# Attention and a dense block on one core: q and k stacked on 128 partitions, loaded by two queues and transposed in one step

## The chip, the cores and the metric

The kernel runs on one core of one Trainium2 chip. The metric is the device time of the kernel in microseconds (us). An engine is named here as the profile names it: PE (TensorE, the matrix engine), ACT (ScalarE), DVE (VectorE), POOL (GpSimd) and SP (SyncE, which in this kernel only issues DMAs). PSUM is the memory that PE writes to, in banks of 2 KB per partition; SBUF holds everything else on the core.

## What is computed

There are 8 batches of 8 heads with 576 tokens of 64 values. For each head, two attentions are added: one over tokens averaged in groups of four, whose result is repeated four times, and one over a band of plus and minus three tokens. The result, 4608 tokens of 512 values, goes through a dense block.

```python
q_d = q.reshape(B, H, Sd, factor, D).mean(axis=3)      # factor 4; k_d and v_d likewise
out_up = np.repeat(sm_attn(q_d, k_d, v_d), factor, axis=2)
mask = np.abs(pos[:, None] - pos[None, :]) < factor
scores = np.where(mask, scale * np.matmul(q, k.transpose(0, 1, 3, 2)), -1000000000.0)
out_local = np.matmul(softmax(scores), v)
x = (out_up + out_local).transpose(0, 2, 1, 3).reshape(B * S, H * D)
h = x @ w_in                                           # 512 -> 2048
out = (h - np.tanh(h)) @ w_out                         # 2048 -> 512
```

(`softmax` stands for the four lines of the reference that subtract the maximum, take the exponential and divide by the sum.)

## The kernel before

**The work.** Two heads make a pair, and there are 32 pairs, four to a batch. The function `attention` (line 373 on) writes down the steps of one pair. q and k of both heads are loaded as 32-bit values by `load_qk` (L286): each of 96 partitions holds six neighbouring tokens of both heads, so each row in memory is 1536 bytes; q and k lie beside each other in one tile `qkn` of four buffers. Two casts (L387) turn them to bf16 in `qr` (two buffers), one for q and one for k; each is 96 partitions by 768 elements. For each of q and k, six transposes on PE (L399) bring 96 x 128 to 128 x 96: q into the first PSUM bank of `ps_ts`, k into the second. After each, a copy on ACT (L405) of 128 x 576 puts the tokens in order into `qk`, with head 0 on partitions 0 to 63 and head 1 on 64 to 127.

From there on nothing is touched by the change: q and k are pooled in two additions (L416, L421), the scores of the first four query blocks (L434) go into the same `ps_ts`, ACT takes the exponential (L457) and DVE masks it (L460); then the scores of the last block and the pooled ones (L434, L449), two exponentials (L466, L469), a mask (L472), the product with v (L483, L489) into `ps_ox`, the division (L498, L500), seven transposes back (L510 to L514), and an addition (L519) into `xT`, the dense block's input. v is loaded by `load_v` (L305 to L311), cast (L346) and pooled on PE for two pairs at a time (L360, L362, copied by L367).

**The dense block.** Blocks of 512 tokens: 16 times four matmuls into one of four banks (L539), tanh on ACT (L547), a subtraction on DVE (L550), then 64 matmuls with w_out (L566) and a store (L577, L580). A block can begin when its batches' pairs are in `xT`. The weights are loaded as 32-bit values into tiles that are still unused (L323 to L332) and cast (L339).

**What sets the order.** `Program` is a planner in Python. Every step is put down with its engine, a cost in ns, what it reads and writes, and a priority; `order` plays the engines against each other and gives one order for each engine, which is then emitted as it is. Every engine works through its list in that order. Some steps (`choice`) name several engines, and the one that is free first in the plan gets them: the casts of q and k do (`REORDER`), with DVE for q and POOL for k after the first four pairs. DMAs are planned as one server with a cost for each kind (`T_QK`, `T_V`, `T_W`). Loads have a high priority: a load of q and k is issued as soon as the casts of four pairs before have freed the buffer, and all loads stand in one chain on SP, in the order in which they were put down. Dense work has the lowest priority on PE and fills what attention leaves. Before the first dense matmul, `filler` puts matmuls on a zero tile (L710) into planned gaps of PE.

The first four pairs use two sets of PSUM banks (`ps_ts`, `ps_ox` and `ps_ts1`, `ps_ox1`) in turn; after them, the second set is given to the dense block and all pairs share the first. In `ps_ts` the order is then: scores and exponential of pair p, transposes and copies of pair p+1, last scores of pair p.

Of the kernel before, what the change touches and what calls it, by code (L numbers as in the profile page):

```python
# [8 lines left out]
FP32 = mybir.dt.float32  # L9
# [141 lines left out]
def kernel(  # L151
# [17 lines left out]
    SCALE = 1.0 / float(D) ** 0.5  # L169
    A6 = 6  # L170
    G6 = S // A6
    QW = 120
# [10 lines left out]
    def fixed(name, shape, dt, n=None, pool=const):  # L183
        if n is None:
            return pool.tile(shape, dt, name=name, tag=name)
        return [pool.tile(shape, dt, name=f"{name}{i}", tag=f"{name}{i}")
                for i in range(n)]

    NQKN, NVST, NVW = 4, 6, 3
    ident = fixed("ident", [128, 128], BF16)  # L190
# [6 lines left out]
    w_out_sb = fixed("w_out_sb", [128, N_FF, Dm], BF16)  # L197
    qkn = fixed("qkn", [G6, 2, 2, A6 * D], FP32, NQKN)
    vst = fixed("vst", [128, 2, NT, 64], FP32, NVST)
    vw = fixed("vw", [128, 4, NT, 65], BF16, NVW)  # L200
    vd = fixed("vd", [128, 2, 4, 65], BF16, NVW)
    qr = fixed("qr", [G6, 2, A6, 128], BF16, 2)
    qk = fixed("qk", [128, 1192], BF16, 2)
# [72 lines left out]

    def load(ns, fn, keys, cost, pri):
        op("SP", ns, fn, writes=list(keys) + ["queue", ("q", keys[0])], pri=pri)
        op("DMA", cost, None, reads=[("q", keys[0])], writes=keys, pri=pri)

    def load_qk(p):

        b, h0, s = p // NP, 2 * (p % NP), p % NQKN
        for i, src in enumerate((q, k)):
            def issue(i=i, src=src):
                nc.sync.dma_start(  # L286
                    out=qkn[s][:, i], in_=src[b, h0:h0 + 2].rearrange(
                        "h (g a) d -> g h (a d)", a=A6))
            load(500, issue, [("qkn", s, i)], T_QK, -30)

    def load_v(p):

        b, j, s = p // NP, p % NP, p % NVST
        t = vst[s]
        for i in range(2):
            h = 2 * j + i
            base = v[b, h]

            def win(tok, n, nt, base=base):
                return bass.AP(tensor=base.tensor, offset=base.offset + tok * D,  # L300
                               ap=[[D, n], [QW * D, nt], [1, D]])

            def issue(h=h, i=i, win=win):
                if b == 0 and h == 0:
                    nc.sync.dma_start(out=t[4:128, i, 0, :], in_=v[b, h, 0:124, :])  # L305
                    nc.sync.dma_start(out=t[:, i, 1:5, :], in_=win(QW - 4, 128, 4))
                elif b == B - 1 and h == H - 1:
                    nc.sync.dma_start(out=t[0:100, i, 4, :], in_=v[b, h, 476:576, :])
                    nc.sync.dma_start(out=t[:, i, 0:4, :], in_=win(-4, 128, 4))
                else:  # L310
                    nc.sync.dma_start(out=t[:, i], in_=win(-4, 128, 5))  # L311
            if (b, h) in ((0, 0), (B - 1, H - 1)):
                def clear(h=h, i=i):
                    part = t[0:32, i, 0, :] if h == 0 else t[96:128, i, 4, :]
                    V.memset(part, 0.0)
                op("DVE", 100, clear, writes=[("vst", s, i)], pri=-99)
            load(1000, issue, [("vst", s, i)], T_V, -30)

# [54 lines left out]
    def attention(p):  # L373
# [5 lines left out]
        pri = 10 * p  # L379
        cold = 1.5 if p < NP else 1.0  # L380


        yield
        for i in range(2):
            dst = qr[s][:, i].rearrange("p a (h d) -> p h a d", d=D)
            srt = qkn[sn][:, i].rearrange("p h (a d) -> p h a d", d=D)
            P.choice([(eng, ns, lambda dst=dst, srt=srt, fn=fn: fn(out=dst, in_=srt))  # L387
                      for eng, ns, fn in REORDER[p >= NEARLY][i]],
                     reads=[("qkn", sn, i)], writes=[("qr", s, i)], pri=pri - 12)


        full = bass.AP(tensor=qk[s].tensor, offset=qk[s].offset,
                       ap=[qk[s].ap[0], [KOFF, 2], [1, 576]])
        for i in range(2):
            b16 = ps[:, i].bitcast(BF16)[:, 0:S]

            def tr(i=i, b16=b16):
                for a in range(A6):
                    T.transpose(b16[:, G6 * a:G6 * a + G6], qr[s][:, i, a, :],  # L399
                                ident[0:G6, 0:G6])  # L400
            if i == 0:
                P.fresh.add(len(P.ops))
            op("PE", 260 * cold, tr, reads=[("qr", s, i), "ident"],
               writes=[(t, i) for t in ts], pri=pri)
            op("ACT", 540, lambda i=i, b16=b16: A.copy(  # L405
                out=full[:, i].rearrange("p (g a) -> p g a", a=A6),
                in_=b16.rearrange("p (a g) -> p g a", a=A6)),
               reads=[(t, i) for t in ts], writes=[("qk", s, i)], pri=pri)
        ts = [(t, i) for t in ts for i in range(2)]
# [20 lines left out]

        def score(t, hh, c):
            rows = slice(64 * hh, 64 * hh + 64)
# [4 lines left out]
        def s1():  # L437
            for t in range(4):
                for hh in range(2):
                    score(t, hh, 512 * hh + QW * t)  # L440

        def s2():
            for hh in range(2):
                score(4, hh, 512 * hh)
            for i in range(2):
                for hh in range(2):
                    rows = slice(64 * hh, 64 * hh + 64)
                    c = 512 * hh + 96 + G * i
                    T.matmul(sc[:, c:c + G], qkd[s][rows, 1, 16 * i:16 * i + 128],  # L449
                             qkd[s][rows, 0, :], start=True, stop=True)  # L450
        qks = [("qk", s, i) for i in range(2)]
        yield
        op("PE", 420 * cold, s1, reads=qks, writes=ts, pri=pri)
        e1 = E[s][:, 0:960].rearrange("p (h c) -> p h c", h=2)
# [9 lines left out]
        yield  # L464
        op("PE", 380 * cold, s2, reads=qks + [("qkd", s)], writes=ts, pri=pri)
        op("ACT", 240, lambda: A.activation(  # L466
            out=e2v, in_=ps[:, :, 0:96], func=AF.Exp, scale=SCALE),
           reads=ts, writes=[("E", s, 1)], pri=pri)
        op("ACT", 560, lambda: A.activation(  # L469
            out=e3, in_=ps[:, :, 96:384], func=AF.Exp, scale=SCALE / 16.0),  # L470
           reads=ts, writes=[("E", s, 2)], pri=pri)
        op("DVE", 220, lambda: V.tensor_tensor(  # L472
# [3 lines left out]

        def outs():
# [25 lines left out]


        px = [po[:, i].bitcast(BF16) for i in range(2)]

# [76 lines left out]
    def dense(kb):  # L585
# [13 lines left out]
        for i in range(16):  # L599
            if kb < NBLK:  # L600
# [5 lines left out]
    ORDER = "p0p1p2p3"  # L606
    T_QK, T_V, T_W, W_PRI, NEARLY = 1150, 900, 2850, -3, NP
    CAST = [("POOL", 700, GP.tensor_copy), ("ACT", 520, A.copy)]
    CAST_V = [[("POOL", 720, GP.tensor_copy), ("ACT", 640, A.copy)],
              [("POOL", 720, GP.tensor_copy)]]  # L610
    any3 = [("DVE", 600, V.tensor_copy), ("ACT", 740, A.copy),
            ("POOL", 860, GP.tensor_copy)]
    REORDER = [[any3, any3], [any3[0:1], any3[2:3]]]
    ADDERS = [[("DVE", 700, 420, V), ("POOL", 1150, 750, GP)],
# [43 lines left out]

    def load_next():

# [3 lines left out]
        if queue:  # L664
            queue.pop(0)
        if nl[0] < NPAIR:
            load_qk(nl[0])
# [14 lines left out]
    for p in range(NPAIR):  # L682
# [10 lines left out]
        if p + 2 < NP:  # L693
            next(work[p + 2])
        load_next()
        if p % NP == NP - 1:
# [45 lines left out]
```

The softmax here doesn't subtract the row's maximum and nothing guards it: scores larger than these inputs give would overflow.

## Time and profile before

| what | value |
|---|---|
| two runs | 370.07 and 371.64 us, median 370.86 us |
| profiled execution: span from its first to its last instruction | 365.3 us (of its time only the span is recorded; the median of the runs is 5.6 us longer) |
| granted PE clock, mean | 0.995 |
| busy: PE, DVE, ACT, POOL | 348.1, 221.2, 222.2, 120.7 us |
| DMA: read from HBM, written | 37.74 MB, 9.44 MB |
| transposes of q and k (L399) | 360 of 96x96 into `ps_ts`, 24 into `ps_ts1` |
| copies of q and k (L405), 128x576 | 64, 640 ns in the median |
| casts of q and k (L387), 96x768 | DVE 541 to 1522 ns, POOL 818 to 2251 ns |
| first dense matmul | 31.72 us |
| last q, k and v load lands | about 180 us |

In lines of the profile, the number after an engine's name is the line of the kernel; `out<-in` are tiles, x is a count, and the bracket at the end gives the idle time of the engine ahead of it and what ended it. SPq stands for SP's instruction queue, which only issues DMAs: the time of such a line is that of the issue and not of the transfer. PEld is PE's loading of the stationary operand. Times are from the span's start.

### The profile page before, as it was taken

The numbers are of one execution on the slowest core, as the hardware profiler recorded it, in microseconds if no ns is written. First come the engines' busy times: TensorE is split into PE (matmuls) and PEld (weight loads), VectorE is DVE, ScalarE is ACT, GpSimd is POOL, SyncE is SP. The second block draws the span as 40 slices with busy tenths as digits, with TensorE's granted clock in tenths as the row PEclk, the third lists the DMA queues.
The fourth block names the chain that finished last, engine by engine and source line by source line (L and its number), as shares of the span: only waits on it lengthen the run. The fifth ranks groups of instructions, "written<-read, shape, count | busy, mean of one in ns | idle before, by whom it ended". The sixth has DMA issues, their size and how long they took to land.

```text
span 365.3 us, 7446 instructions
## 1 busy us (share of the span) xinstructions
PE 348.1 (95%) x2908; PEld 181.3 (50%) x2908; DVE 221.2 (61%) x362; ACT 222.2 (61%) x406; POOL 120.7 (33%) x156
## 2 busy tenths in 40 slices
PE   7777999999999999999999999999999999999995
PEld 3454455556555555555555555444444444444442
DVE  5786775688989988779777667434334334334300
ACT  3686986679787877777877774434434434434321
POOL 6744666674656564555635220000000000000000
PEclk9899999999999999999999999999999999999999
DMA  8999999999999986576400000010010011011012
GB/s 202 235 390 286 257 258 259 212 264 227 240 207 234 206 182 183 148 190 148 126 31 2 30 31 31 29 57 31 29 57 31 29 52 37 29 42 46 29 62 82
DMA packets 64816, 47.65 MB, mean 130 GB/s; under 512 B 43790, under 2 KB 56078, under 8 KB 64782
## 3 DMA queue, kind: packets, MB, share of 16 engines
q1 hardware_dynamic: 64782, 47.19, 54.1%
q8 instruction: 22, 0.36, 0.5%
q14 instruction: 12, 0.10, 0.1%
HBM read 37.74 MB, written 9.44 MB: 129 GB/s over the span
## 4 chain that ended last, share of the span: by engine, by line
PE 81%; DVE 6%; ACT 5%; DMA 3%; POOL 2%; issue 2%; SPq 0%; ACTq 0%; DVEq 0%; POOLq 0%
PE ps_hy_527 L566 9%; PE ps_hy_528 L566 9%; PE ps_hy_525 L539 8%; PE ps_hy_525 L566 8%; PE ps_hy_526 L539 8%; PE ps_hy_528 L539 7%; PE ps_hy_527 L539 7%; PE ps_hy_526 L566 7%; PE ps_ts L399 4%; PE ps_ts L434 3%; PE ps_ox L360 3%; DMA qkn_75<-in_k_dram 2%; ACT qk_91 L405 2%; PE ps_ox L483 2%; PE ps_ox L514 2%
## 5 line engine op out<-in xcount | busy, mean ns | idle before, releaser
L539 PEld LDWEIGHTS <-w_in_sb 128*128 128x128 bf16 x576 | 52.5, 98 | 59.6 <-issue 1.3
L566 PEld LDWEIGHTS <-gT_103 128*128 128x128 bf16 x320 | 28.9, 97 | 30.7
L566 PEld LDWEIGHTS <-gT_104 128*128 128x128 bf16 x256 | 23.5, 98 | 25.8
L405 ACT COPY qk_90<-ps_ts 128x576 bf16<-128x576 bf16 x32 | 19.5, 644 | 6.7 <-PE ps_ts L399 6.6
L416 POOL TENSOR_TENSOR half<-qk_91 128x576 f32<-128x576 bf16 x16 | 19.0, 1188 | 13.6 <-ACT qk_91 L405 10.9
L405 ACT COPY qk_91<-ps_ts 128x576 bf16<-128x576 bf16 x28 | 17.5, 640 | 7.3 <-PE ps_ts L399 7.3
L566 PE MATMUL ps_hy_525<-w_out_sb,gT_103 128*128 128x512 bf16 x80 | 20.9, 380 | 0.0
L566 PE MATMUL ps_hy_526<-w_out_sb,gT_103 128*128 128x512 bf16 x80 | 20.9, 380 | 0.0
L566 PE MATMUL ps_hy_527<-w_out_sb,gT_103 128*128 128x512 bf16 x80 | 20.7, 380 | 0.0
L566 PE MATMUL ps_hy_528<-w_out_sb,gT_103 128*128 128x512 bf16 x80 | 20.4, 380 | 0.0
L416 POOL TENSOR_TENSOR half<-qk_90 128x576 f32<-128x576 bf16 x14 | 16.3, 1167 | 10.2 <-ACT qk_90 L405 10.2
L500 DVE TENSOR_TENSOR ln_99<-ps_ox,r_97 128x896 bf16<-128x896 f32 x16 | 17.4, 1089 | 0.5
L457 ACT ACTIVATE E_95<-ps_ts 128x960 bf16<-128x960 f32 x16 | 15.6, 977 | 3.3 <-PE ps_ts L434 3.2
L566 PE MATMUL ps_hy_527<-w_out_sb,gT_104 128*128 128x512 bf16 x64 | 17.3, 380 | 0.0
L566 PE MATMUL ps_hy_526<-w_out_sb,gT_104 128*128 128x512 bf16 x64 | 17.0, 380 | 0.0
L566 PE MATMUL ps_hy_525<-w_out_sb,gT_104 128*128 128x512 bf16 x64 | 16.9, 380 | 0.0
L566 PE MATMUL ps_hy_528<-w_out_sb,gT_104 128*128 128x512 bf16 x64 | 16.8, 380 | 0.0
L399 PEld LDWEIGHTS <-qr_89 96*128 96x128 bf16 x192 | 11.3, 100 | 9.7 <-issue 4.9
L500 DVE TENSOR_TENSOR ln_100<-ps_ox,r_98 128x896 bf16<-128x896 f32 x14 | 15.3, 1092 | 0.5
L399 PE MATMUL ps_ts<-ident,qr_88 96*128 96x96 bf16 x192 | 12.4, 213 | 3.1 <-DVE qr_88 L387 2.2
L399 PE MATMUL ps_ts<-ident,qr_89 96*128 96x96 bf16 x168 | 11.2, 206 | 4.2 <-ACT qk_91 L405 3.7
L457 ACT ACTIVATE E_96<-ps_ts 128x960 bf16<-128x960 f32 x14 | 13.6, 973 | 2.1 <-PE ps_ts L434 1.8
(218 smaller groups left out, 887.9 us busy)
## 6 DMA issues: line engine op xcount, KB each, us to landing
out_dram<-y_108 SPq DMA_DIRECT2D x12, 256.0 KB, 2.0
out_dram<-y_109 SPq DMA_DIRECT2D x12, 256.0 KB, 2.0
out_dram<-y_110 SPq DMA_DIRECT2D x12, 256.0 KB, 2.0
qkn_72<-in_q_dram SPq DMA_DIRECT2D x8, 288.0 KB, 7.7
qkn_72<-in_k_dram SPq DMA_DIRECT2D x8, 288.0 KB, 7.5
qkn_73<-in_q_dram SPq DMA_DIRECT2D x8, 288.0 KB, 5.2
qkn_73<-in_k_dram SPq DMA_DIRECT2D x8, 288.0 KB, 6.1
qkn_74<-in_q_dram SPq DMA_DIRECT2D x8, 288.0 KB, 6.9
```

The lines of the kernel that those rows point to most:

```text
L360: T.matmul(pv[:, 0, :], pick[:, t, :], vw[w][:, :, t, 0:64], start=(t == 0), stop=(t == NT - 1))
L399: T.transpose(b16[:, G6 * a:G6 * a + G6], qr[s][:, i, a, :], ident[0:G6, 0:G6])
L405: op("ACT", 540, lambda i=i, b16=b16: A.copy(out=full[:, i].rearrange("p (g a) -> p g a", a=A6), in_=b16.rearrange("p (a g) -> p g a", a=A6)),
L416: eng.tensor_tensor(out=half, in0=four[:, :, :, 0:2], in1=four[:, :, :, 2:4], op=ALU.add)
L434: T.matmul(sc[:, c:c + NQ[t]], qk[s][rows, k0:k0 + 128], qk[s][rows, QW * t:QW * t + NQ[t]], start=True, stop=True)
L457: op("ACT", 870, lambda: A.activation(out=e1, in_=ps[:, :, 0:480], func=AF.Exp, scale=SCALE), reads=ts, writes=[("E", s, 0)], pri=pri)
L483: T.matmul(po[:, hh, 65 * t:65 * t + 65], E[s][:, c:c + 128], vw[w][:, 2 * jj + hh, t, :], start=True, stop=True)
L500: op("DVE", 1010, lambda: V.tensor_tensor(out=ln[s].rearrange("p n (h d) -> p h n d", d=D), in0=blocks[:, :, :, 0:64], in1=r[s].unsqueeze( ...
L514: T.transpose(px[0][:, QW * t:QW * t + n], ln[s][0:n, t, :], ident[0:n, 0:n])
L539: T.matmul(ps_hy[slot], w_in_sb[:, dc, fc * 128:(fc + 1) * 128], xT[dc][:, kb * 512:kb * 512 + 512], start=(dc == 0), stop=(dc == N_DC - 1))
L566: T.matmul(ps_hy[slot], gT[g][:, fc, ts * 128:ts * 128 + 128], w_out_sb[:, fc, :], start=(fc == 0), stop=(fc == N_FF - 1))
```

## The change

q goes to partitions 0 to 63 and k to partitions 64 to 127 of one tile, nine neighbouring tokens to a partition, so that a row in memory is 2304 bytes. q is loaded by SP's queue as before and k by ACT's queue; each queue has its own chain in the plan. The cast takes q and k together: one step of 128 x 1152 after the first four pairs (DVE or POOL, whichever is free first in the plan), and two of 128 x 576, one for each head, in the first four pairs (DVE, ACT or POOL). Nine transposes of 128 x 128 take q and k together into both banks, as one step on PE. They are followed by one copy of 128 x 1152 on ACT, in the first four pairs by two of 128 x 576. The planned costs are new. `XB` marks the pairs from which on a DMA would transpose in PE's place; it is 32, the number of pairs, so no pair takes that branch, and with it the rule in `load_next` and the `after` of the loads do nothing (no step writes the key `fl`).

```diff
-    A6 = 6
-    G6 = S // A6
+    A9 = 9
+    G9 = S // A9
+    XB = NPAIR
...
-    qkn = fixed("qkn", [G6, 2, 2, A6 * D], FP32, NQKN)
+    qkn = fixed("qkn", [128, 2, A9 * D], FP32, NQKN)
-    qr = fixed("qr", [G6, 2, A6, 128], BF16, 2)
+    qr = fixed("qr", [128, A9, 128], BF16, 2)
+    qT = fixed("qT", [128, A9, 128], BF16, 2)
+    lnT = fixed("lnT", [128, 7, 128], BF16, 2)
...
-    def load(ns, fn, keys, cost, pri):
-        op("SP", ns, fn, writes=list(keys) + ["queue", ("q", keys[0])], pri=pri)
+    def load(ns, fn, keys, cost, pri, after=[], eng="SP"):
+        op(eng, ns, fn, reads=after, writes=list(keys) + [(eng, "queue"), ("q", keys[0])],
+           pri=pri)
         op("DMA", cost, None, reads=[("q", keys[0])], writes=keys, pri=pri)
...
     def load_qk(p):
         b, h0, s = p // NP, 2 * (p % NP), p % NQKN
-        for i, src in enumerate((q, k)):
-            def issue(i=i, src=src):
-                nc.sync.dma_start(
-                    out=qkn[s][:, i], in_=src[b, h0:h0 + 2].rearrange(
-                        "h (g a) d -> g h (a d)", a=A6))
-            load(500, issue, [("qkn", s, i)], T_QK, -30)
+        for i, (src, eng, name) in enumerate(((q, nc.sync, "SP"), (k, nc.scalar, "ACT"))):
+            def issue(i=i, src=src, eng=eng):
+                eng.dma_start(
+                    out=qkn[s][64 * i:64 * i + 64], in_=src[b, h0:h0 + 2].rearrange(
+                        "h (g a) d -> g h (a d)", a=A9))
+            load(500, issue, [("qkn", s, i)], T_QK, -30, [("fl", p - 2)], name)
...
-        for i in range(2):
-            dst = qr[s][:, i].rearrange("p a (h d) -> p h a d", d=D)
-            srt = qkn[sn][:, i].rearrange("p h (a d) -> p h a d", d=D)
-            P.choice([(eng, ns, lambda dst=dst, srt=srt, fn=fn: fn(out=dst, in_=srt))
-                      for eng, ns, fn in REORDER[p >= NEARLY][i]],
-                     reads=[("qkn", sn, i)], writes=[("qr", s, i)], pri=pri - 12)
+        dst = qr[s].rearrange("p a (h d) -> p h a d", d=D)
+        srt = qkn[sn].rearrange("p h (a d) -> p h a d", d=D)
+        for h in range(2) if p < NEARLY else (slice(0, 2),):
+            P.choice([(eng, ns, lambda dst=dst[:, h], srt=srt[:, h], fn=fn: fn(
+                out=dst, in_=srt)) for eng, ns, fn in REORDER[p >= NEARLY]],
+                     reads=[("qkn", sn, 0), ("qkn", sn, 1)],
+                     writes=[("qr", s, h)] if p < NEARLY else
+                     [("qr", s, 0), ("qr", s, 1)], pri=pri - 12)
...
-        for i in range(2):
-            b16 = ps[:, i].bitcast(BF16)[:, 0:S]
-            def tr(i=i, b16=b16):
-                for a in range(A6):
-                    T.transpose(b16[:, G6 * a:G6 * a + G6], qr[s][:, i, a, :],
-                                ident[0:G6, 0:G6])
...
-            op("PE", 260 * cold, tr, reads=[("qr", s, i), "ident"],
-               writes=[(t, i) for t in ts], pri=pri)
-            op("ACT", 540, lambda i=i, b16=b16: A.copy(
-                out=full[:, i].rearrange("p (g a) -> p g a", a=A6),
-                in_=b16.rearrange("p (a g) -> p g a", a=A6)),
-               reads=[(t, i) for t in ts], writes=[("qk", s, i)], pri=pri)
+        if xbar:
...
+        else:
+            b16 = ps.rearrange("p n c -> p (n c)").bitcast(BF16)[:, 0:2 * S]
+            def tr():
+                for a in range(A9):
+                    T.transpose(b16[:, 128 * a:128 * a + 128], qr[s][:, a, :], ident)
+            P.fresh.add(len(P.ops))
+            op("PE", 520 * cold, tr, reads=[("qr", s, 0), ("qr", s, 1), "ident"],
+               writes=[(t, i) for t in ts for i in range(2)], pri=pri)
+            for i in range(2) if p < NEARLY else (slice(0, 2),):
+                op("ACT", 650 if p < NEARLY else 1150, lambda i=i: A.copy(
+                    out=full.rearrange("p i (g a) -> p i g a", a=A9)[:, i],
+                    in_=b16.rearrange("p (a i g) -> p i g a", a=A9, i=2)[:, i]),
+                   reads=[(t, i) for t in ts for i in range(2)],
+                   writes=[("qk", s, i)] if p < NEARLY else
+                   [("qk", s, 0), ("qk", s, 1)], pri=pri)
...
-    T_QK, T_V, T_W, W_PRI, NEARLY = 1150, 900, 2850, -3, NP
+    T_FLIP, T_IN, T_OUT = 1500, 1300, 1000
+    T_QK, T_V, T_W, W_PRI, NEARLY = 800, 900, 2850, -3, NP
...
-    any3 = [("DVE", 600, V.tensor_copy), ("ACT", 740, A.copy),
-            ("POOL", 860, GP.tensor_copy)]
-    REORDER = [[any3, any3], [any3[0:1], any3[2:3]]]
+    REORDER = [[("DVE", 420, V.tensor_copy), ("ACT", 680, A.copy),
+                ("POOL", 700, GP.tensor_copy)],
+               [("DVE", 720, V.tensor_copy), ("POOL", 1250, GP.tensor_copy)]]
...
-        if nl[0] < NPAIR:
+        if nl[0] < NPAIR and (nl[0] < XB + 2 or nl[0] <= p + 3):
```

## The prediction

> **What bounds the kernel now.** I read the 40 slices of the page first, then busy time by stage, then the order in time around the lines that the diff touches, then the waits.
>
> ```profile
> span 365.3 us, 7446 instructions
> ...
> PE   7777999999999999999999999999999999999995
> ...
> DMA  8999999999999986576400000010010011011012
> ```
>
> TensorE (PE) is full from slice 5 on; the DMA engines are full for the first 14 slices and nearly idle from slice 21. The stages (busy us of each engine, then clock, DMA share, GB/s):
>
> ```profile
> 0.00:32.00 32.00, 23.42 (x246) 13.03 (x247) 21.78 (x49) 19.52 (x36) 18.96 (x36) 0.95 1.06 272
> 32.00:65.00 33.00, 32.38 (x301) 17.50 (x300) 22.90 (x36) 26.74 (x49) 20.60 (x26) 1.00 1.15 265
> 65.00:125.00 60.00, 58.94 (x656) 33.69 (x655) 51.33 (x81) 47.71 (x91) 36.87 (x44) 1.00 1.18 227
> 125.00:216.00 91.00, 87.79 (x995) 50.42 (x995) 69.67 (x115) 69.78 (x128) 44.27 (x52) 1.00 0.45 114
> 216.00:366.00 150.00, 145.54 (x722) 66.69 (x720) 55.55 (x84) 58.46 (x104) 0.00 (x0) 1.00 0.11 41
> ```
>
> So there are two regimes. Up to 31.72 us, where the first dense matmul starts, data and the four first pairs set the pace. After it PE has dense work to put between the attention pieces, so the end moves only by PE work and PE gaps; an attention step that merely comes later costs nothing. From 216 us there is no attention left and the change has nothing to touch.
>
> Now the gaps at the transposes (L399), in order of time:
>
> ```profile
> 102.73 0.67 PE L399 MATMUL ps_ts<-ident,qr_88 96*128 96x96 bf16 x12
> 103.49 1.18 ACT L405 COPY qk_90<-ps_ts 128x576 bf16<-128x576 bf16 x2
> ...
> 108.46 0.42 PE L399 MATMUL ps_ts<-ident,qr_89 96*128 96x96 bf16 x6
> ...
> 109.16 0.63 ACT L405 COPY qk_91<-ps_ts 128x576 bf16<-128x576 bf16 x1
> ...
> 109.84 0.41 PE L399 MATMUL ps_ts<-ident,qr_89 96*128 96x96 bf16 x6 [0.32 <-ACT qk_91 L405]
> ```
>
> Where the k half is issued right behind the q half, twelve transposes run through. Where the planner puts other work between them, the k half starts 51 ns after the copy of the q half has ended, though it writes the other bank. PE issues in order, so all of PE stands still. I took the distance from each matmul's start to the next: nine such places after L489 (411, 509, and seven of about 646 ns, where 30 is usual) and two after L539 (471 where 216 is usual). That is (411 + 509 + 7x646 - 9x30 + 2x255) ns = 5.7 us.
>
> Two views for the queues: the waits of 31.7 to 225 us, and SyncE's issues.
>
> ```profile
> POOL qr_88 L387 <- PE ps_ts L399: 20.5, 8, 3.1
> ...
> POOL qr_89 L387 <- PE ps_ts L399: 11.7, 9, 3.8
> ```
> ```profile
> 43.84 3.50 SPq L286 DMA_DIRECT2D qkn_75<-in_q_dram  x1
> 47.43 0.40 SPq L286 DMA_DIRECT2D qkn_75<-in_k_dram  x1
> ...
> 125.04 0.33 SPq L286 DMA_DIRECT2D qkn_75<-in_q_dram  x1
> ```
>
> The first: the casts wait for the transposes to free qr, so they run up to two pairs ahead of their use. The second: an issue takes 0.33 us on a free queue and up to 3.50 us on a full one.
>
> **The change part by part.** A pair takes 6.4 us (odd pairs' gaps 12.83 us apart); 28 pairs run beside dense work.
>
> 1. One transpose step instead of two. PE has no second half to hold back, so the eleven gaps go: -5.7 us. What is late next is the one copy of 128x1152. The exps of 128x576 and 128x960 took about 0.65 and 0.975 us, so 1152 is an estimate of 1.14 us. From first transpose to last copy the old order took 1.94 us (together) or 2.47 us (apart); the new one 0.50 + 0.26 + 1.14 = 1.90 us. So the scores that follow aren't later. If they were, each place would cost what the gap did, 0.5 us.
> 2. Nine 128x128 transposes for twelve 96x96. Start to start: 96x96 43 ns, 120x120 53, 128x128 (L510, L511) 56 to 60. No row has nine of 128. Ends: 9x43 and 9x60 against 12x43, so -0.13 to +0.02 us a pair, -3.6 to +0.6 us in all. I take 56, the same shape: -0.01 a pair, -0.3 us.
> 3. One cast of 128x1152 (DVE or GpSimd) for two of 96x768. DVE's took 0.56 us alone and up to 1.5 beside GpSimd, GpSimd's 0.82; half as much again is 0.84 to 2.25, or 1.23 us. Priced at nothing: the two pairs of lead (about 6 us) hide it. Without the lead each late cast would hold PE as the one at 57.43 us did, 0.57 us. In the first four pairs there are two casts of 128x576, and both need both loads.
> 4. Copies on ScalarE (ACT): 1.18 to 1.14 us a pair, nothing.
> 5. k's 32 issues leave SyncE and come to ACT. On SyncE they delay nobody but later loads. On ACT each takes 0.33 us or more, and stands in order: it must wait until the cast of four pairs before has freed the slot of qkn, and behind it stand copies, exps and tanhs, on which PE waits. ACT is idle 12.3 us of 60 in 65 to 125, 1.3 us a pair. The floor, 28x0.33 = 9.2 us, fits in; ends nothing and 14 pairs x 2.0 us (rival C). I take +0.7 us, two issues that hit a copy.
> 6. Loads. At saturation a q or k load lands 1.2 to 1.5 us behind the one before. In the trace's packet records of 8 to 35 us, 1536 B packets (96 partitions) took 102 ns, 2048 B ones (the weights, 128 partitions) 86. An engine moved 12 of the former a load, 1.22 us; now it has 8 of 2304 B, at the weights' rate 97 ns, 0.77 us. Over the eight loads of the first four pairs at most 8x0.45 = 3.6 us are gained. Against it: k has its own queue, so k of pairs 4 to 7 is asked for as soon as the casts of pairs 0 to 3 are done, and goes ahead of v, q and w_in still queued on SyncE: 4x1.2 = 4.8 us of traffic earlier than needed. The end of the stage is not only data: v of pair 3 landed at 18.29 us, then DVE worked from 19.16 to 31.67 nearly without rest on normalising and adding for four pairs. Between -3.6 and +4.8 I take -0.5 us, k of pair 0 (landed 5.39, q 3.83) coming a little sooner.
> 7. The DMA-transpose branch: XB is NPAIR, so no pair takes it, and no such DMA is issued: nothing.
>
> Sum: -5.7 - 0.3 + 0.7 - 0.5 = -5.8 us.
>
> The trace's rows speak for a shorter load in point 6. [...] No run here has 64 partitions yet.
>
> The profiled execution's span is 365.3 us; the runs' median, 370.86, has 5.6 us more around it, which the change doesn't touch. So 370.86 - 5.8 = 365.1 us.
>
> **The rivals.**
> A. The start shortens too: the loads reach the weights' rate and the first dense matmul comes 3 us earlier: 362.1 us. For it: DMA share 1.06 in the first stage. Against: DVE's 12.5 us tail behind the last landing.
> B. The start gets longer: k of pairs 4 to 7 goes ahead and v and q come up to 4.8 us later: 365.6 + 4.8 = 370.4 us.
> C. Slower: ACT is held at k's issue. If the chip makes ACT wait as long as SyncE does on a full queue (mean of q's issues from 17.5 to 65 us: 1.99 us), 14 pairs from 32 to 125 us are hit. ACT's idle 1.3 us a pair is the point from which it decides; scattered as it is, half may be usable: 14 x (2.0 - 0.65) = 19 us, 365 + 19 = 384 us; if all is usable 14 x 0.7 = 10, 375 us. Between them 379 us. Against: ACT's queue would hold only 128 rows a pair, where v alone puts 1280 on SyncE's.
> D. The gaps change place: PE waits for the joint cast or joint copy at the same eleven places: 370.9 - 0.3 = 370.6 us. Against: the lead of point 3.
>
> **How the numbers follow.** Forecast 0.45, A 0.25, B 0.10, C 0.12, D 0.08. The forecast's own range, from the ends of points 2 and 5, is 362 to 368 us. For 8 in 10 the range takes in A with the transposes' lower end (358.5) and the lower part of C (376). This kernel can tell about 2% from no change: 363.4 and 378.3 us. Faster: A and a little of the forecast, 0.30; slower: most of C, 0.11; within: 0.59.
>
> **What would show it.** Right: no transposes that wait for a copy in the middle of a pair, distances at L399 of 53 to 60 ns, one copy of 1.1 to 1.2 us a pair, ACT's k issues near 0.33 us, first dense matmul at 30 to 32 us, PE as full as now. Wrong: k issues over 1.3 us on ACT, PE waiting for casts or for ACT's exps, a first dense matmul after 34 us, or a time outside the range.

## The result, and the profile after

The changed kernel takes 387.47 us (median of 386.61 and 388.33) against 370.86 us: 1.047 times as long, with an interval of 1.036 to 1.058. The forecast was 365.1 us, the range 358.5 to 376.0. So the sign was wrong, and the time lies outside the range. Ratios leave out disturbed runs that the medians can include; where the two differ (e1, whose four runs lie between 372.3 and 381.6 us, and e4) I go by the ratio, of which 1% is 3.7 us. By the ratio the change costs 17.4 us; the two medians are 16.6 us apart.

Four lines of the page of the changed kernel (its span, and the 40 slices for PE, its clock and the DMA engines):

```profile
span 384.9 us, 7115 instructions
...
PE   5575769795999899999999999999999999999996
...
PEclk9886988997899999999999999999999999999999
DMA  8999999999966686968974000010010100101012
```

Before, PE was full from slice 5 on. Now it has holes up to slice 10, about 96 us, and its clock falls in and behind them. From there on PE's row looks as before. The same stages as before (busy us of PE, PEld, DVE, ACT and POOL, then PE's clock, DMA share, GB/s):

```profile
0.00:32.00 32.00, 18.25 (x171) 10.78 (x173) 14.49 (x39) 14.92 (x25) 12.42 (x30) 0.87 1.05 218
32.00:65.00 33.00, 25.54 (x184) 13.48 (x187) 19.30 (x31) 21.49 (x42) 13.01 (x20) 0.81 1.13 260
65.00:125.00 60.00, 51.61 (x494) 30.16 (x502) 35.07 (x54) 36.99 (x63) 31.22 (x36) 0.91 0.97 191
125.00:216.00 91.00, 88.34 (x965) 51.91 (x981) 64.77 (x106) 69.98 (x122) 57.26 (x59) 1.00 0.73 153
```

All five engines do less in the first two stages than they did (DVE 21.78 and 22.90 us before, now 14.49 and 19.30), while the DMA engines are as busy as before and, in the first stage, move less: 218 GB/s where it was 272. That is a kernel that waits for data. PE ran at half its clock for 31 us in all, before for 3.4.

The loss can be dated by the start of the nth of the 1152 weight loads of the dense block: the first came at 38.5 us (before 30.3), the 128th behind it at 98.7 (73.5), the 512th at 241.5 (222.1), the last at 380.5 (360.9). The kernel was 8 us late at the first, 25 us late at 100 us, and won 6 us of that back by 240 us.

### The profile page after: what moved, and what is told of

The parts are those of the page before. It is cut to its first block, busy times and chain, and to the rows that moved or that the text cites. A ratio compares the mean times of both kernels' runs of the same rounds, so it can differ in the third digit from the quotient of the medians.

```text
span 384.9 us, 7115 instructions
## 1 busy us (share of the span) xinstructions
PE 347.7 (90%) x2757; PEld 184.7 (48%) x2806; DVE 203.7 (53%) x336; ACT 218.2 (57%) x380; POOL 123.6 (32%) x152
## 4 chain that ended last, share of the span: by engine, by line
PE 73%; DMA 18%; SPq 3%; issue 2%; ACT 2%; DVE 1%; ACTq 0%; DVEq 0%
PE ps_hy L589 29%; PE ps_hy L616 28%; DMA vst<-in_v_dram 8%; DMA qkn<-in_q_dram 3%; DMA gT<-in_moe_w_out_dram 3%; PE ps_ts L418 3%; PE ps_ts L454 3%; DMA qkn<-in_k_dram 2%; SPq L319 2%; PE ps_ox L514 2%; DMA xT<-in_moe_w_out_dram 2%; PE ps_ox L368 2%; PE ps_ox L564 2%; PE ps_ox L520 2%; PE ps_ox L560 1%
## 5 line engine op out<-in xcount | busy, mean ns | idle before, releaser
L589 PE MATMUL ps_hy<-xT,w_in_sb 128*128 128x512 bf16 x554 | 144.3, 385 | 2.9 <-DVE xT L569 1.2
L600 DVE TENSOR_TENSOR gT<-ps_hy,u 128x512 bf16<-128x512 f32 x144 | 97.2, 688 | 89.3 <-ACT u L597 85.0
L616 PE MATMUL ps_hy<-w_out_sb,gT 128*128 128x512 bf16 x551 | 139.3, 382 | 2.0 <-issue 1.0
L597 ACT ACTIVATE u<-ps_hy 128x512 f32<-128x512 f32 x144 | 83.9, 599 | 83.6 <-PE ps_hy L589 76.1
L616 PEld LDWEIGHTS <-gT 128*128 128x128 bf16 x576 | 53.6, 98 | 58.6 <-issue 1.3
L423 ACT COPY qk<-ps_ts 128x1152 bf16<-128x1152 bf16 (+1 forms) x36 | 36.2, 1018 | 17.5 <-PE ps_ts L418 13.1
L436 POOL TENSOR_TENSOR half<-qk 128x576 f32<-128x576 bf16 x29 | 35.6, 1227 | 14.2 <-ACT qk L423 13.0
L396 POOL CAST qr<-qkn 128x1152 bf16<-128x1152 f32 (+1 forms) x27 | 29.8, 1105 | 22.7 <-PE ps_ts L418 15.3
L531 DVE TENSOR_TENSOR ln<-ps_ox,r 128x896 bf16<-128x896 f32 x32 | 34.9, 1092 | 1.1
L483 ACT ACTIVATE E<-ps_ts 128x960 bf16<-128x960 f32 x32 | 31.0, 973 | 7.7 <-PE ps_ts L454 7.2
L627 ACT COPY y<-ps_hy 128x512 f32<-128x512 f32 x36 | 21.2, 588 | 17.5 <-PE ps_hy L616 16.6
L500 DVE TENSOR_TENSOR E<-E,mask 128x192 bf16<-128x192 bf16 x32 | 11.9, 371 | 21.9 <-ACT E L494 21.7
```

Source lines behind the costliest of these rows:

```text
L396: P.choice([(eng, ns, lambda dst=dst[:, h], srt=srt[:, h], fn=fn: fn(out=dst, in_=srt)) for eng, ns, fn in REORDER[p >= NEARLY]], reads=[( ...
L423: op("ACT", 650 if p < NEARLY else 1150, lambda i=i: A.copy(out=full.rearrange("p i (g a) -> p i g a", a=A9)[:, i], in_=b16.rearrange("p ( ...
L436: eng.tensor_tensor(out=half, in0=four[:, :, :, 0:2], in1=four[:, :, :, 2:4], op=ALU.add)
L483: op("ACT", 870, lambda: A.activation(out=e1, in_=ps[:, :, 0:480], func=AF.Exp, scale=SCALE), reads=ts, writes=[("E", s, 0)], pri=pri)
L531: op("DVE", 1010, lambda: V.tensor_tensor(out=ln[s].rearrange("p n (h d) -> p h n d", d=D), in0=blocks[:, :, :, 0:64], in1=r[s].unsqueeze( ...
L589: T.matmul(ps_hy[slot], w_in_sb[:, dc, fc * 128:(fc + 1) * 128], xT[dc][:, kb * 512:kb * 512 + 512], start=(dc == 0), stop=(dc == N_DC - 1))
```

## The experiments

Three theories stood at the start. **Q**: the second queue costs, because k of later pairs goes ahead of data that are needed sooner (overtaking), or because ACT is held while it waits to issue (the hold). **L**: the layout costs; a load to 64 partitions runs more slowly than the one to 96 did. **P**: the joint cast, transposes and copy cost. Times of the first dense weight load and spans are of the profiled execution.

| run | what it is | us | ratio to before, interval | span | first dense |
|---|---|---|---|---|---|
| after | the changed kernel | 387.5 | 1.047, 1.036 to 1.058 | 384.9 | 38.5 |
| e1 | after, one queue | 377.3 | 1.011, 1.005 to 1.017 | 373.5 | 34.2 |
| e2 | before, two queues | 379.1 | 1.026, 1.021 to 1.030 | 377.0 | 40.3 |
| e3 | after, ACT issues k of four pairs only | 378.1 | 1.022, 1.018 to 1.026 | 376.2 | |
| e4 | before, one transpose step | 364.8 | 0.984, 0.980 to 0.988 | 362.0 | 28.1 |
| e5 | e1, plan with 1350 | 369.5 | 1.001, 0.998 to 1.005 | 368.5 | 29.2 |
| e6 | e1, loads to 128 partitions | 356.2 | 0.966, 0.962 to 0.970 | 355.6 | 29.2 |
| e7 | e1, k overtakes | 379.8 | 1.030, 1.026 to 1.035 | 376.9 | |
| e8 | e1, ACT held | 380.5 | 1.031, 1.025 to 1.038 | 378.4 | 35.9 |
| e9 | after, plan with 1350 | 381.2 | 1.032, 1.028 to 1.037 | 379.7 | 34.6 |
| e10 | e5, quarters | 364.4 | 0.987, 0.982 to 0.993 | 362.8 | 28.3 |
| e11 | e6 with the reference's function | 364.7 | 0.988, 0.983 to 0.993 | 363.5 | 28.8 |
| e12 | e11, two queues | 372.6 | 1.010, 1.006 to 1.013 | 370.5 | 30.7 |
| e13 | e7 and e8 together | 383.4 | 1.038, 1.035 to 1.040 | 382.2 | |
| e14 | four heads together | 640.4 | 1.734, 1.729 to 1.738 | 638.1 | |
| e15 | e14, rows listed otherwise | 362.6 | 0.985, 0.980 to 0.991 | 364.1 | 35.7 |

**e1_one_queue**: the changed kernel with k issued by SP behind q.

```diff
-        for i, (src, eng, name) in enumerate(((q, nc.sync, "SP"), (k, nc.scalar, "ACT"))):
+        for i, (src, eng, name) in enumerate(((q, nc.sync, "SP"), (k, nc.sync, "SP"))):
```

> The changed kernel with k issued from SyncE again, behind q; layout, joint cast, joint transposes and planned costs stay. Theory Q (the second queue is the cause: k's loads of later pairs overtake what is needed first, and ScalarE stands in order behind issues that wait for older DMAs): 366 to 372 us, first dense matmul at 30 to 33 us. Rival L (the layout is the cause: 64-partition packets of 2304 B took 148 to 173 ns where those of 1536 B took 87 to 102, so q and k land late on any queue): 382 us or more, first dense matmul at 37 us or more. Rival P (the joint cast and joint transposes make the first pairs late): 382 us or more too.

The time lies between the two cases. By ratio 3.6% (13.5 us) of the change is the second queue, and 1.1% above before is left although the transposes are joint. By the median of its four runs e1 is at 1.021 instead. Then the second queue's price is 2.6%, what is priced against e1 below (e3, e7, e8, e13) is 1 point less, and the 64 partitions (e6) are 1 point more. Three comparisons below do without e1 (e2 with before, e9 with e5, e12 with e11) and put the second queue at 2.2 to 3.1%.

**e2_old_two_queues**: the kernel before, only k's loads moved to ACT's queue with a chain of its own. **e3_act_first_four**: the changed kernel with k on ACT for pairs 0 to 3 only.

```diff
+        kq = (nc.scalar, "ACT") if p < NP else (nc.sync, "SP")
...
```

> The kernel before with one edit: k is issued from ScalarE on its own queue. Layout, casts, transposes and costs stay those of before. Theory Q: 383 to 390 us, first dense matmul 5 to 9 us later than before. Rivals L and P: 368 to 374 us, as before, since neither the layout nor the joint steps are there.

> The changed kernel with k issued from ScalarE for the first four pairs only (no wait for a cast there), and from SyncE behind q from pair 4 on. Theory Q: no k overtakes and ScalarE is held by hardly any issue, so 366 to 374 us. Rivals L and P: 382 us or more.

Both times lie between their cases: no theory alone explains them. The second queue costs 2.6% (9.5 us) in the old layout as well. By the ratios about a third of its price in the changed kernel (1.1 of 3.6%) is paid by the first four pairs; with e1's interval of 0.6% to each side that share is rough.

**e4_old_joint_step**: the kernel before with all twelve transposes of a pair as one step, and both copies behind it.

```diff
-            op("PE", 260 * cold, tr, reads=[("qr", s, i), "ident"],
-               writes=[(t, i) for t in ts], pri=pri)
+        op("PE", 520 * cold, tr, reads=[("qr", s, 0), ("qr", s, 1), "ident"],
+           writes=[(t, i) for t in ts for i in range(2)], pri=pri)
...
```

> The kernel before with one edit: the twelve transposes of q and k are one step on the matrix engine, with both copies behind it; loads, layout and casts stay. It tests the first term of the sum by itself. If the eleven waits of the second half for the first half's copy cost what their gaps show: 364 to 367 us. If other waits take their place: 369 to 373 us.

0.984 is 5.9 us less, and from 31.7 to 225 us no matmul at L399 starts over 200 ns after another one: the gaps are gone. All 28 pairs run their twelve transposes through, as these two do:

```profile
105.19 0.67 PE L399 MATMUL ps_ts<-ident,qr 96*128 96x96 bf16 x12
110.93 0.68 PE L399 MATMUL ps_ts<-ident,qr 96*128 96x96 bf16 x12
```

So the joint transposes are what the prediction took them for, in size too. That all of the 5.9 us is the gaps isn't shown, since e4's dense block also begins 2.2 us earlier. The joint cast and copy aren't in e4; e6, which has them all, is at 0.966, so P falls.

**e5_plan_1350**: e1 with the planner's cost of a q or k load at 1350 ns instead of 800 (`T_QK`).

> The changed layout on one queue (k behind q on SyncE, as in the run with one queue, 377.3 us), with one number changed: the planner's cost of a q or k load is 1350 ns instead of 800, which is nearer to the 1.3 to 1.5 us by which those loads landed behind each other. Theory M (part of the loss is that each engine's order was made for data that come earlier than they do, so that engines stand in front of late data): 366 to 372 us. Theory D (the data themselves are late, and no order mends that): 374 to 379 us.

The orders had been made for data that come earlier than they do; 0.9% of e1 is that. With an honest plan and one queue the layout takes what the joint step gains: 1.001.

**e6_all_partitions**: e1 with each load of q or k to all 128 partitions, a row of nine tokens of one head in each. Rows, bytes, number of loads and steps stay. It computes another function: the transposes mix q and k of the two heads.

```diff
-                    out=qkn[s][64 * i:64 * i + 64], in_=src[b, h0:h0 + 2].rearrange(
-                        "h (g a) d -> g h (a d)", a=A9))
+                    out=qkn[s][:, i], in_=src[b, h0:h0 + 2].rearrange(
+                        "h (g a) d -> (h g) (a d)", a=A9))
```

> The changed layout on one queue, but each load goes to all 128 partitions: the two heads of q lie on the two halves, and those of k likewise in the second half of the row. Same tile, same row of 2304 bytes, same bytes, same steps and costs; q and k of the heads are mixed up by it, so another function is computed. Theory H (64-partition destinations make the packets slow): packets of 2304 B take 95 to 115 ns instead of 150 to 180, loads land 0.8 to 1.0 us behind each other, time 363 to 369 us. Theory S (it's the size of the row, or HBM): packets stay at 150 ns and more, time 373 to 378 us.

The first two stages of e1, and then of e6, columns as above:

```profile
0.00:32.00 32.00, 21.61 (x206) 14.32 (x208) 17.26 (x43) 18.89 (x33) 16.20 (x35) 0.84 1.05 249
32.00:65.00 33.00, 26.65 (x206) 13.52 (x210) 20.75 (x34) 21.87 (x39) 12.76 (x17) 0.95 1.13 246
```

```profile
0.00:32.00 32.00, 20.68 (x228) 12.64 (x232) 20.98 (x48) 20.38 (x38) 19.16 (x38) 0.89 1.01 314
32.00:65.00 33.00, 32.54 (x302) 18.06 (x305) 25.85 (x39) 27.77 (x50) 19.12 (x23) 1.00 1.12 329
```

At the same DMA share 314 and 329 GB/s pass where e1 has 249 and 246. In the packet records of 8 to 35 us a packet of 2304 bytes took 180 ns in the median in e1 (173 in the changed kernel) and 95 ns in e6; k of pair 3 landed at 19.25 and 13.31 us. The same of the page's DMA issues, with the median from issue to landing at the end, e1 and then e6:

```profile
qkn<-in_q_dram SPq DMA_DIRECT2D x32, 288.0 KB, 7.5
qkn<-in_k_dram SPq DMA_DIRECT2D x32, 288.0 KB, 7.3
```

```profile
qkn<-in_q_dram SPq DMA_DIRECT2D x32, 288.0 KB, 3.0
qkn<-in_k_dram SPq DMA_DIRECT2D x32, 288.0 KB, 4.8
```

So L holds: the 64 partitions cost 4.4% (16 us) more than 128. With e5, whose plan fits the slower loads, in e1's place it is 3.5% (13 us). The time is 7 us below the case that was expected of L.

**e7_sp_overtakes**: e1, but k of later pairs has a chain of its own on SP and goes ahead as in the changed kernel; ACT issues nothing. **e8_hold_only**: e1, where ACT issues a transfer of 16 KB that nobody reads at the place of each k load from the fifth pair on.

```diff
-            load(500, issue, [("qkn", s, i)], T_QK, -30, [("fl", p - 2)], name)
+            load(500, issue, [("qkn", s, i)], T_QK, -31 if i and p >= NP else -30, [("fl", p - 2)], name)
...
```
```diff
+        if p >= NP:
+            op("ACT", 500, lambda: nc.scalar.dma_start(out=tiny, in_=q[0, 0, 0:64, :]),
+               reads=[("cast", p - NP)], writes=[("ACT", "queue")], pri=-30)
...
```

> The changed kernel with k issued by SyncE, but still in a chain of its own in the plan, so that k of pair 4 and later goes ahead of v, weights and q as in the changed kernel; ScalarE issues nothing and is never held. Theory O (what the second queue costs is the overtaking): 383 to 390 us, as the changed kernel. Theory A (it's ScalarE held at its issues): 371 to 379 us, as with one queue in order.

> Every q and k load is issued by SP in one chain as in e1_one_queue (377.3 us, 1.0106 times before); ScalarE issues besides, for each pair from the fifth on and at the place where the changed kernel puts its k load, one transfer of 16 KB into a tile of its own, which nobody reads. The order of the real loads stays; only ScalarE is held at the issue. Q-hold (ScalarE waits at its issues, 0.60 us each and 16 us in all in the changed kernel): 382 to 386 us, ratio 1.025 to 1.035. Q-overtake alone (the hold hidden by the loads): 376 to 379, ratio 1.005 to 1.015. 28 further transfers of 16 KB, by the rows about 0.1 us of packets on each engine in sum for each three, are worth under 1 us.

Each alone costs 2.0 to 2.1% over e1 (3.4 and 4.9 us by the spans). e7 lies between its cases, 0.8 us above that of the hold. Its k of pairs 4 to 6 landed at 19.83, 21.48 and 24.85 us and v of pair 3 at 27.84, so it does overtake as the changed kernel does. e8's ratio is in the range expected of the hold, its time 2 us below. e8's hold can be seen in the timeline of ACT (start, duration, then the line; the bracket is the idle time ahead):

```profile
73.13 0.61 ACT L379 CAST vd<-ps_ox 128x512 bf16<-128x512 f32 x1
77.53 0.49 ACTq L300 DMA_DIRECT2D tiny<-in_q_dram  x1
78.06 0.97 ACT L487 ACTIVATE E<-ps_ts 128x960 bf16<-128x960 f32 x1 [4.33 <-DMA tiny<-in_q_dram]
```

ACT stood for 3.79 us in front of a transfer of 16 KB, and the exponential behind it came that much later. But this isn't the changed kernel's wait: all small transfers go to one tile, and the issue at 77.53 us waited for the one before it, which landed at 77.51. In all, e8's ACT was held for 7.7 us before 125 us, and the changed kernel's for 16.2 (time from the end of ACT's work to the start of an issue). So e8 shows that issues on ACT cost, and doesn't measure the changed kernel's hold.

**e9_two_queues_1350**: the changed kernel with e5's plan.

> The changed kernel with only its planner's figure for a load raised from 800 to 1350, as e5_plan_1350 did it for one queue (369.5 us, ratio 1.0012). Q (the second queue costs by overtaking and by the hold, whatever the plan): 376 to 383, ratio 1.02 to 1.04, so 7 to 13 above e5. Plan alone (the second queue cost only since the orders were made for data that come earlier): 368 to 372, ratio 1.0 to 1.01.

3.1% (11.5 us) above e5: the second queue costs under either plan.

**e10_quarters**: e5 with q on partitions 0 to 31 and 64 to 95, k on the others, each load as two transfers.

```diff
+                for x in range(2):
+                    at = 64 * x + 32 * i
+                    eng.dma_start(out=qkn[s][at:at + 32], in_=rows[32 * x:32 * x + 32])
...
```

> e5_plan_1350 (one queue, 369.5 us) with q on partitions 0 to 31 and 64 to 95 and k on 32 to 63 and 96 to 127: each load is two transfers of 32 partitions, the copy out of PSUM is two of 128x576 instead of one of 128x1152 (each 0.64 against 1.12 us together, some 5 us of ScalarE in all, mostly beside other work). L (the halves of the partitions limit a transfer; neighbours in a queue that reach both halves work side by side): packets nearer to the 93 ns of e6_all_partitions than to its 160 to 180, the landing of k of pair 3 before 17 us and 362 to 368 us, ratio 0.98 to 1.0. If a small set of partitions is slow by itself: packets still 150 ns or more, twice the issues (some 0.4 us each, 64 more) on SP: 370 to 378, ratio 1.0 to 1.025.

The time and 0.987 are in the range of L, but its two signs didn't come: packets took 148 ns (8 to 35 us), nearer to e5's 172 than to e6's 95, and k of pair 3 was in at 17.36 us (e5: 18.21), not before 17. So neighbours in the queue that lie in both halves made these packets a little faster, far less so than one load over all partitions did. How much of the 5 us below e5 that is stays open, since e10 also splits the copy out of PSUM in two.

**e11_all_by_heads**: e6's loads, and the reference's function: 36 transposes of 64x64 in place of 9. **e12_all_two_queues**: e11 with k on ACT.

```diff
+                for i, a, h in [(i, a, h) for i in range(2) for a in range(A9)
+                                for h in range(2)]:
+                    r, c = slice(64 * h, 64 * h + 64), 64 * (A9 * i + a)
+                    T.transpose(b16[r, c:c + 64], qr[s][r, a, 64 * i:64 * i + 64],
+                                ident[r, r])
...
```

> The loads of e6_all_partitions (one queue, each q or k load to all 128 partitions, a row of nine tokens of one head in each), and the reference's function: the two heads of a pair lie on partitions 0 to 63 and 64 to 127, so each block of 64 tokens is transposed by itself, 36 transposes of 64x64 in place of 9 of 128x128. The two heads' score matmuls of e6, on the two halves of TensorE's rows, start 3 to 4 ns apart, two in some 50 ns; if the two heads' transposes go side by side likewise, 18 steps of some 30 ns are 0.54 us a pair against 0.50: 355 to 360 us, ratio 0.96 to 0.975. If they go one after the other, 36 x 30 ns = 1.08 us a pair, 32 pairs x 0.58 = 18 us more on TensorE: 370 to 376, ratio 1.0 to 1.02. L's price by a kernel that computes the same as e1_one_queue: some 17 to 21 us below its 377.3.

> e11_all_by_heads with k issued by ScalarE, as the changed kernel issues it: the layout without its slow packets, the second queue kept. Q (the second queue costs by itself, by the hold and by overtaking): 8 to 12 us above e11, as with the old layout (e2, +8) and with the changed one (after against e1, +10); 365 to 370 us if e11 is at 357, ratio 0.985 to 1.005. If the queue costs only where the packets are slow: within 3 us of e11.

Neither of the two cases of e11 came out. The two heads' transposes do go side by side (3 to 4 ns apart, a step every 31.7 ns), the packets are those of e6 (96 ns), and yet e11 is 8 us slower. By distances of starts, a pair's transposes cost 0.12 us more in themselves (35x16.1 against 8x55.7 ns), 0.09 on the way in (309 against 216 ns behind a dense matmul) and 0.07 on the way out (125 against 56): 0.28 us, 28 pairs, 7.8 us. That fits the lag behind e6, which grows from -0.4 us at the first dense weight load to 7.9 at the 512th. In e12 the second queue costs 2.2% (8 us), with ACT held for 6.7 us in place of the changed kernel's 16.2: it costs with fast packets too.

**e13_overtake_and_hold**: e7's and e8's edits together, all real loads on SP.

> All real loads on SP, k of the later pairs ahead of others by a chain of its own as in e7_sp_overtakes (379.8 us, ratio 1.0304), and ScalarE held at 28 small transfers as in e8_hold_only (380.5, 1.0313); e1_one_queue, with neither, was at 377.3 and 1.0106. If the two add up by the ratios: 1.0106 + 0.020 + 0.021 = 1.051, 387 to 389 us, the changed kernel's 1.047. If each hides the other or a third thing makes up the difference: 379 to 384, ratio 1.03 to 1.04.

The second case came out: 383.4 us and 1.038 are 2.7% over e1, less than the sum of the ratios (4.1%), though the spans add up (3.4 + 4.9 = 8.3 us, measured 8.7). The changed kernel has 3.6%, with an interval of 1.1% to each side. So most of the second queue's price comes back when k overtakes and ACT issues. How it divides between the two isn't shown, as e13's ACT was held for only 5.1 us before 125 us, and the rest (2.7 us by the spans) isn't resolved.

**e14_quad** and **e15_quad_rows_first**: loads over 128 partitions, of two heads that aren't neighbours; four heads are transposed together, q and then k, 128x128. e15 lists the same rows in another order.

```diff
-                    ap=[[2 * S * D, 2], [A9 * D, G9], [1, A9 * D]]))
+                    ap=[[A9 * D, G9], [2 * S * D, 2], [1, A9 * D]]))
...
```

> 128-partition loads as in e11_all_by_heads (364.7 us), each of two heads that are not neighbours; four heads are transposed together, q and then k, in 18 transposes of 128x128 for two pairs, as many a pair as in the changed kernel, so TensorE never changes to 64 rows for them. Everything else is computed as in the reference. If e11's 8 us above e6 are TensorE's (0.13 us a pair in the transposes themselves, some 0.07 to 0.09 at each change between 64 and 128 rows, 32 pairs): 355 to 360, ratio 0.96 to 0.975. If the price of the layout itself was the 12.6 us: 363 to 367, ratio 0.985 to 0.995. Against it: the first pair waits for the loads of two, some 2 us at the start, and the two pairs' copies stand together.

> e14_quad with the rows of a load listed groups of tokens first and the two heads inside, so that partition 2g + h holds group g of head h. If the order of that list was what made e14's loads slow: k of pair 3 lands before 15 us as in e11_all_by_heads (13.5), and then as expected for e14: 355 to 360 us, ratio 0.96 to 0.975, if e11's 8 us above e6 are TensorE's changes between 64 and 128 rows; 363 to 367, ratio 0.985 to 0.995, if not. If a list of two dimensions is slow in either order: 600 us and more.

e14 failed as a test, on something else. Its first stage:

```profile
0.00:32.00 32.00, 13.41 (x53) 5.71 (x54) 3.74 (x25) 4.61 (x7) 5.75 (x21) 0.65 0.18 58
```

DMA share 0.18 of 16 engines is 2.9 engines; its packets took 94 ns, as fast as e6's, but k of pair 0 landed at 15.2 us. With the 64 groups first (e15) it landed at 6.1 us. So the order of the list decided how much of the engines these loads used. Between 5 and 25 us the 2304-byte packets kept 2.1 engines busy; why isn't shown, since no record names a packet's engine. e15's ratio, 0.985, is at the lower end of the case in which e11's 8 us are not TensorE's (its 362.6 us are just below that case), so by its own terms the run speaks against TensorE. The dates of the dense block say something else. At the first dense weight load it is 6.5 us behind e6 (35.7 against 29.2 us: the first pair waits for the loads of two), at the 64th 8.7, and at the 512th still 8.7. So without the 64-row transposes no drift is left: e15 loses its time at the start, e11 pair by pair. That supports the account of e11's 8 us.

e4, e10, e11 and e15, which compute the reference's function, lie 1.2 to 1.6% below the kernel before, with intervals that overlap one another.

## Why the prediction was wrong, point by point

Point 1 (the joint step, -5.7 us) was right: e4 gives -5.9, and the 6 us that the changed kernel won back between 100 and 240 us fit it. The scores didn't come later: from 31.7 to 225 us they start 2.3 us behind the first transpose in the median, and before 2.6. This is a pair in the middle of the changed kernel, transposes, joint copy and first scores:

```profile
102.88 0.67 PE L418 MATMUL ps_ts<-ident,qr 128*128 128x128 bf16 x9
...
103.64 1.12 ACT L423 COPY qk<-ps_ts 128x1152 bf16<-128x1152 bf16 x1 [0.39 <-PE ps_ts L418]
105.14 0.10 PEld L454 LDWEIGHTS <-qk 64*128 64x128 bf16 x2 [0.42 <-issue]
```

Points 2 and 4 were right: 55.8 ns from transpose to transpose (56 taken) and copies of 1.12 us (1.14). Point 3 held, with casts of 0.87 (DVE) and 1.14 us (POOL); one late cast made PE wait 0.70 us, at 42.91 us. Point 7 held.

**Point 6 failed, on the rate of the loads.** The step read 102 ns for 1536 bytes on 96 partitions and 86 for 2048 bytes on 128, and put the better rate down to the longer packet. The rows differed in two things, and the other one mattered: 2304 bytes took 95 ns on 128 partitions (e6) and 173 to 180 on 64 (the changed kernel, e1). The order of the rows in memory isn't it: e15 takes the rows of two heads in turn, as e1 does, and its packets took 95 ns. With a load's packets spread evenly over the page's 16 engines (an estimate, as no record names a packet's engine), an engine needed 8 x 180 ns = 1.44 us for a load, where the same estimate gives 1.22 for before and the prediction had 0.77. In e5's first four loads (landed at 4.50, 5.95, 7.14 and 8.59 us) one is 1.2 to 1.5 us apart from the next, and k of pair 3 landed at 18.21 us, before at 15.60. Where the term had a gain of up to 3.6 us, there was a loss. The trace of before held the warning: 15 bytes per ns to 96 partitions beside 24 to 128, at sizes that differ by a third.

Why 64 partitions are slower isn't shown. That they are, e6 against e1 shows: 95 against 180 ns for the same bytes.

**Rival B's mechanism, inside point 6, was right and too small.** k of pairs 4 to 6 landed at 17.65, 21.83 and 26.33 us, ahead of v of pair 3 (24.34, before 18.29) or of the first w_in (31.01, before 20.96). It was priced at 4.8 us for four loads once; at the real packets a load is dearer, and it goes on in later stages. By itself it costs 2.0% by the ratios (e7).

**Point 5 failed on what an issue on ACT costs.** It took 0.33 us an issue and two hits, 0.7 us. An issue took 0.60 us, which is the layout's doing and not ACT's: q's on SP took 0.60 us too, and in the old layout k's on ACT took 0.32 (e2). And ACT was held for 16.2 us before 125 us, up to 3.3 us at a time. This is ACT's timeline in the changed kernel, with two lines of PE:

```profile
9.59 0.60 ACTq L294 DMA_DIRECT2D qkn<-in_k_dram  x1
10.23 0.64 ACT L423 COPY qk<-ps_ts 128x576 bf16<-128x576 bf16 x1 [2.81 <-DMA qkn<-in_k_dram]
...
17.75 0.60 ACTq L294 DMA_DIRECT2D qkn<-in_k_dram  x1
18.40 0.33 ACT L494 ACTIVATE E<-ps_ts 128x192 bf16<-128x192 f32 x1 [1.98 <-DMA qkn<-in_k_dram]
...
53.09 0.60 ACTq L294 DMA_DIRECT2D qkn<-in_k_dram  x1
...
54.29 1.12 ACT L423 COPY qk<-ps_ts 128x1152 bf16<-128x1152 bf16 x1
...
55.46 0.27 PE L454 MATMUL ps_ts<-qk 64*128 64x96 bf16 x2 [2.17 <-ACT qk L423]
...
90.41 0.60 ACTq L294 DMA_DIRECT2D qkn<-in_k_dram  x1
91.06 0.33 ACT L494 ACTIVATE E<-ps_ts 128x192 bf16<-128x192 f32 x1 [3.13 <-DMA qkn<-in_q_dram]
...
92.43 0.23 PE L514 MATMUL ps_ox<-vw,E 128*128 128x65 bf16 x1 [3.48 <-DVE E L500]
```

In two places the hold can be followed to PE. Behind the issue at 53.09 us the copy came late, and PE stood 2.17 us for it; behind the one at 90.41 the exponential and its mask on DVE (L500) came late, and PE stood 3.48 us.

The argument was that ACT's queue would hold few rows. No record tells how full a queue is; "free" and "full" were my reading of issues of 0.33 and up to 3.50 us. What the trace of the changed kernel shows is a wait for an earlier transfer. Its 180 issues use eight semaphores, on which the trace marks their landings, in turn over both queues (22 or 23 issues each). For 129 issues the landing of the transfer before it on the same semaphore is recorded, and none of them starts ahead of that landing. Nine of ACT's ten waits of over 0.1 us before 125 us end 0.02 to 0.10 us behind it: the issue at 9.59 us follows k of pair 2, landed at 9.49; the one at 53.09 a w_out load of SP's, landed at 53.01; the one at 90.41 a v load, landed at 90.31. So rival C's hold is what happened, without a full queue being shown. Its price (10 to 19 us, taken as 14) is near the 13.5 us that the second queue costs, but that is luck, since B's price is in the 13.5. What the changed kernel's hold costs alone isn't measured; e8's 2.1% belong to a shorter hold of another kind.

The sum that would have been right, by ratios: -5.9 us for the joint step (e4); +9.8 for the layout with its plan (e1 against e4), of which 3.5 are the planner's 800 ns; +13.5 for the second queue (the changed kernel against e1): +17.4 us, measured 1.047 x 370.86 - 370.86 = 17.4. The three make it up by how they are defined; each has its own run, and the last two share e1's uncertainty.

The lower clock may add to it: 0.81 in 32 to 65 us, where it had been 1.00. No run holds the clock while the data are late, so how much of the 17.4 us is the clock's stays open.

## What to carry to other kernels

Before taking a packet's rate from another row, match the destination's partitions as well as the size: here, on loads that set the pace, packets of 2304 bytes took 95 ns to all 128 partitions (e6) and 180 to 64 (e1), so the 64 partitions cost more than the longer row was to bring. A DMA issue on an engine that computes was also a wait in that engine's order, in the changed kernel of up to 3.3 us, and nine times in ten until an earlier transfer, of either queue, had landed; it wasn't the issue time of 0.60 us alone. Move one thing at a time: here a gain of 5.9 us (e4) came in one edit with two losses that were each larger.

## What the runs showed of the hardware

- 2304-byte packets: 94 to 100 ns to 128 partitions (e6, e11, e12, e14, e15), 148 to alternating quarters (e10), 169 to 181 to halves (e1, e3, e5, e7, e9, the changed kernel; medians of 8 to 35 us). Packets of 256 bytes (v, to all partitions) in the same stretch took 18 ns in e6 and 28 in e1 and the changed kernel: beside the slow loads they were slower too.
- Issuing a load took 0.60 us at the least to 64 partitions, on SP as on ACT (e1, the changed kernel), and 0.32 to 0.33 to 96 or 128 (before, e2, e6, e12).
- Transposes of 64x64 on the two halves of PE's rows started 3 to 4 ns apart, a step every 31.7 ns, but the way in and out of them behind and before other matmuls took 0.09 and 0.07 us more (309 against 216 ns, 125 against 56; e11 against e6).
- The same rows, with the dimension of two heads listed first (e14), kept 2.9 of 16 DMA engines busy in the first 32 us, and the kernel took 640 us instead of 363 (e14, e15).
